# Paced weight preparation from step 0 to step 22 of the experts, and pools opened a step sooner, in a one-core attention, expert and gated-product kernel

## The chip, the cores and the metric

The kernel runs on one core of a Trainium2 chip. The metric is the device time of one execution in microseconds (us), median of several runs. The kernel before takes 837.07 us (three runs: 836.84, 837.07 and 842.2).

## The reference

Three layers follow each other. Linear attention gives x (2304 tokens, 512 features); a top-1 mixture of 8 experts replaces it; a gated product of three matrices gives the output.

```python
x = attn(q, k, v, w_phi)                      # linear attention, exp features
logits = x @ w_gate + modality_bias[modality_id]
e_idx = argmax(logits, axis=1)                # one expert for a token
for e in range(8):
    h = maximum(x[mask_e] @ w1[e], 0)         # 512 -> 1024
    out[mask_e] = gate_w * (h @ w2[e])        # 1024 -> 512
x = out
return ((x @ w_a) * (x @ w_b)) @ w_out        # 512 -> 1536 -> 512
```

The weights of the last layer come as 64-bit floats, laid out as pairs of 32-bit words.

## The kernel before

Every product is made of three matmuls on a high and a low part of both operands (`mm3`, lines 54 to 56). So each operand is split: ScalarE (ACT) copies it to the matmul's type, and VectorE (DVE) subtracts this copy from it.

**The experts** (`Moe.run`) work on four tiles of 608 tokens. A tile has eight steps. Steps 0 to 3 make the hidden layer: PE writes `hp`, ACT makes `hh` (L602), DVE makes `hl` (L603). Steps 4 to 7 make the output: PE writes `yp` from `hh` and `hl`, ACT copies it to `y` (L615). Together these are 32 steps, numbered 0 to 31. Each step has one slice of expert weights `s`, loaded by SyncE (SP, L555) and split two steps ahead into `wh` (ACT, L563) and `wl` (DVE, L564).

**The preparation** of the gated layer's weights runs beside the experts, as side jobs of these steps. The gated layer (`Moe2`) has 12 slices of weights; 10 of them (`NPRE`) are prepared during the experts, each in two halves, so there are 20 halves. A half has three jobs. `fetch` is a load of `raw` by SP (L700; three buffers). `clamp` is an absolute value on ACT (L708) and a maximum on GpSimd (POOL, L709). `narrow` is five DVE operations (L720, L722, L724, L725, L727) that turn the 64-bit words into 32-bit floats `wsum`. After the second half, `park` adds four small DVE operations (L736 to L739), and then splits the slice in two pieces of 1024 and 1280 columns: ACT writes `whi` (L744; one buffer), DVE subtracts it (L745), and SP stores both parts to DRAM as `wsc` (L746, L747).

A table `side` says at which step a job is handed to the scheduler. Inside `conv`, `high_priority(offset=-LOWP)` places the job's instructions as if they were written LOWP (200) instructions later; `issue_after(mo.act)` and `issue_after(mo.dve)` keep them behind the expert instruction that was handed over last on ACT and on DVE. Each engine then works through its instructions in the order so fixed.

**The boundary.** `open_first` is a side job too. It closes the preparation's buffers and opens the gated layer's in their place: `f_t`, `f_s` and `f_w0`. Into these go the prepared weights of slice 0, loaded back from `wsc` (`fw`, L774), and the sums and splits of the first tokens (`terms`: DVE `ysum` L806, ACT `yh` L791, DVE `yl` L792). All of them therefore wait until the last store of the preparation has left its buffer. Behind this stands a branch that all engines take (L1037; extra tiles, not needed with these inputs), and then the gated layer runs: PE makes the products `abp`, ACT copies them out (`pc`, L888). The last two slices of weights are prepared there, with loads of `raw` that SP issues behind the loads of the second slice's `fw`.

Of the kernel before, what the change touches and what calls it, by code (L numbers as in the profile page):

```python
# [37 lines left out]
NPRE = 10  # L38
LOWP = 200
LOWR = 80  # L40
LOWP2 = 60
# [7 lines left out]
def f32(ap):  # L49
    return ap.bitcast(F32)  # L50
# [213 lines left out]
def consts(nc, pool, keep, w_phi, w_gate):  # L264
    c = {}
    ident = c["ident"] = keep.tile([P, P], F32, name="ident")
    w = c["wp"] = pool.tile([P, P], F32, name="wp")
    nc.scalar.dma_start(out=w[0:64, :], in_=w_phi)
    nc.scalar.dma_start(out=w[64:128, :], in_=w_phi)
    make_identity(nc, ident)  # L270
    mask = c["mask"] = pool.tile([P, 2], F32, name="mask")
    wg = c["wg"] = pool.tile([P, 4, 16], F32, name="wg")
    nc.gpsimd.memset(wg, 0.0)
    src = w_gate.rearrange("(p h d) e -> h d p e", h=2, d=64)
    for h in range(2):
        rows = slice(64 * h, 64 * h + 64)
        nc.gpsimd.memset(mask[rows, h:h + 1], 0.0)
        nc.gpsimd.memset(mask[rows, 1 - h:2 - h], -1000.0)
        nc.gpsimd.dma_start(out=wg[rows, :, 8 * h:8 * h + 8], in_=src[h])
    return c  # L280
# [250 lines left out]
class Moe:  # L531
# [26 lines left out]
    def splitw(self, T, j):  # L558
        nc = self.nc
        src = T.pop(("st", j))  # L560
        hi = self.p_w.tile([P, 8, P], F32R, tag="h", name="wh")
        lo = self.p_w.tile([P, 8, P], F32R, tag="l", name="wl")
        nc.scalar.copy(hi, src)  # L563
        self.dve = nc.vector.tensor_sub(lo, src, f32(hi)).ins  # L564
        T["w", j] = (hi, lo)

# [360 lines left out]
def low(tc, step):  # L927
    def run():
        with tc.high_priority(offset=-LOWR):
            step()  # L930

    return run


@with_exitstack
def trn_kernel(ctx, tc, qk, v, vt, w_phi, mod_id, w_gate, bias, wm, wf, out):
    nc = tc.nc
    f64 = wf.dtype == mybir.dt.int64
    if f64:
        wf = wf.bitcast(I32)  # L940
    keep = ctx.enter_context(tc.tile_pool(name="keep", bufs=1))
    rpool = ctx.enter_context(tc.tile_pool(name="route", bufs=1))
    dpool = ctx.enter_context(tc.tile_pool(name="dram", bufs=1, space=bass.MemoryType.DRAM))
    xs = [dpool.tile([HALF, DM], F32, name=f"xs{i}") for i in range(2)]
    wsc = [[dpool.tile([P, 2304], F32, name=f"wsc{f}{j}") for j in range(2)] for f in range(Moe2.NF)]
    tl = dict(reuse_waits="tile")
    with ExitStack() as actx:
        cpool = actx.enter_context(tc.tile_pool(name="const", bufs=1))
        wkpool = actx.enter_context(tc.tile_pool(name="rwork", bufs=1))
        lgp = [(cpool, keep)[i].tile([P, NG, E], F32, name=f"lgp{i}") for i in range(2)]  # L950
        with tc.tile_pool(name="warm_ps", bufs=1, space=PSUM) as wps:
            z = cpool.tile([P, 512], BF16, name="warm")
            nc.vector.memset(z, 0.0)
            wz = wps.tile([P, 512], F32, name="warmp")
            for i in range(NWARM):
                nc.tensor.matmul(wz, z[:, :P], z, start=i == 0, stop=i == NWARM - 1)
        cst = consts(nc, cpool, keep, w_phi, w_gate)
        cst["warm"] = z
        at = Attn(nc, tc, actx, cst, qk, v, vt, xs, lgp)
        at.load(0)  # L960
        for r in range(9):
            if r + 1 < 8:
                at.load(r + 1)
            if r == 2:
                bs = bias_load(nc, cpool, keep, bias, mod_id)
                routes = [Route(tc, rpool, lgp[i], bs[i], i) for i in range(2)]
                rsteps = routes[0].steps(wkpool, at.ps_c, "c", at.first)
                rsteps = [low(tc, st) for st in rsteps[:6] + [lambda: routes[0].back(at.ps_q, "q")]]
            if r == 0:
                order = ExitStack()  # L970
                order.enter_context(tc.manual_schedule(engines={mybir.EngineType.PE}))
            at.round(r, {4: {2: rsteps[:1]}, 5: {0: rsteps[1:2], 2: rsteps[2:4]}, 6: {2: rsteps[4:5]}, 7: {0: rsteps[5:6]},
                         8: {0: rsteps[6:]}}.get(r, {}) if r > 2 else {})
            if r == 8:
                order.close()
    with ExitStack() as mctx:
        ps_t = mctx.enter_context(tc.tile_pool(name="ps_t", bufs=2, space=PSUM, **tl))
        ps_l = mctx.enter_context(tc.tile_pool(name="ps_l", bufs=3, space=PSUM, **tl))
        ypool = ctx.enter_context(tc.tile_pool(name="y", bufs=1, **tl))
        y = [ypool.tile([P, 4, YC], F32, name=f"y{i}") for i in range(2)]  # L980
        m2 = Moe2(nc, tc, wf, wsc, y, routes, out, f64)
        mo = Moe(nc, tc, mctx, cst, xs, wm, y, ps_l, ps_t)
        tiles = [(rt, t) for rt in routes for t in range(NTMIN)]
        rctx = ExitStack()
        cv = []
        nts = []
        ws = {}

        cctx = ExitStack()
        cv.append(cctx.enter_context(tc.tile_pool(name="cv", bufs=1, **tl)))  # L990

        def close_work():
            rctx.close()
            top = rpool.tile([1, 1], I32, name="top")
            n = slice(3 * NTMAX, 3 * NTMAX + 1)
            nc.vector.tensor_tensor(out=top, in0=routes[0].meta[:, n], in1=routes[1].meta[:, n], op=ALU.max)
            nts.append(nc.values_load(top[:, :], min_val=0, max_val=NTMAX))

        wk1 = rctx.enter_context(tc.tile_pool(name="rwork1", bufs=1, **tl))
        rs = routes[1].steps(wk1, ps_t, "t")  # L1000
        side = {}
        for f, k in enumerate((0, 0, 2, 4, 4, 8, 8)):
            side.setdefault(k, []).append(low(tc, rs[f]))
        side[9] = [close_work]

        def conv(f, half, job):
            def run():
                with tc.high_priority(offset=-LOWP), tc.issue_after(mo.act), tc.issue_after(mo.dve):
                    job(half)
            return run  # L1010

        K0, K1 = 2, len(tiles) * mo.NJ - 4
        for f in range(NPRE):
            fetch, clamp, narrow = m2.jobs(f, cv[0], 2, 3, 2)
            for half in range(2):
                k = K0 + (K1 - 2 - K0) * (2 * f + half) // (2 * NPRE)
                for i, job in enumerate((fetch, clamp, narrow)):
                    side.setdefault(k + i, []).append(conv(f, half, job))
        ts, src0 = {}, []

        def first():
            src, ts[0] = m2.terms(0, m2.p_s, ts.get(0), src0[0] if src0 else None)
            src0.append(src)

        def open_first():
            cctx.close()
            m2.p_t[0] = ctx.enter_context(tc.tile_pool(name="f_t", bufs=Moe2.NT0, **tl))
            m2.p_s = ctx.enter_context(tc.tile_pool(name="f_s", bufs=1, **tl))
            m2.p_w[0] = ctx.enter_context(tc.tile_pool(name="f_w0", bufs=1, **tl))
            ws[0] = m2.weights(0)  # L1030
            with tc.high_priority(offset=-LOWP):
                first()

        side.setdefault(K1, []).append(open_first)
        tc.mark_branch_hint_location("extra", "LikelyTaken", engines=ENGINES)
        mo.run(tiles, side, at)
        with tc.If(nts[0] > NTMIN, label="extra"):  # L1037
            n = slice(3 * NTMAX, 3 * NTMAX + 1)
            for rt in routes:
                extra(tc, mo, rt, nc.values_load(rt.meta[:, n], min_val=0, max_val=NTMAX))  # L1040
            first()
    cv.append(ctx.enter_context(tc.tile_pool(name="cv2", bufs=1, **tl)))
    side = {}
    for f in range(NPRE, Moe2.NF):
        for i, job in enumerate(m2.jobs(f, cv[1], 1, 2, 2)):
            for half in range(2):
                side.setdefault(2 * (f - NPRE) + i, []).append(lambda job=job, half=half: job(half))
    ps_l = ctx.enter_context(tc.tile_pool(name="ps_l2", bufs=2, space=PSUM, **tl))
    ps_a = ctx.enter_context(tc.tile_pool(name="ps_a2", bufs=1, space=PSUM, **tl))
    m2.pools(ctx, ps_a, ps_l)  # L1050
    m2.p_o = cv[1]
    m2.run(ws, ts, src0[0], side)
# [58 lines left out]
```

## Time and profile before

| | us |
|---|---|
| median of three runs | 837.07 |
| the profiled execution, its own time | 834.7 |
| its span in the trace | 832.9 |
| PE busy | 801.8 (96%) |
| DVE busy | 600.9 (72%) |
| ACT busy | 376.0 (45%) |
| POOL busy | 135.9 (16%) |

PE is TensorE's matmul queue, and PEclk (or the clock of a window) is the share of full speed that the chip granted it: 1.00 is 2.4 GHz, about 0.5 is 1.2 GHz. A timeline row gives the start, the duration, the engine, the line and the operation, with the tile written and the tiles read; in brackets stands the engine's idle time ahead of the row and what ended it. The experts run from about 163 to 388 us.

### The profile page before, as it was taken

The numbers are of one execution on the slowest core, as the hardware profiler recorded it, in microseconds if no ns is written. First come the engines' busy times: TensorE is split into PE (matmuls) and PEld (weight loads), VectorE is DVE, ScalarE is ACT, GpSimd is POOL, SyncE is SP. The second block draws the span as 40 slices with busy tenths as digits, with TensorE's granted clock in tenths as the row PEclk, the third lists the DMA queues.
The fourth block names the chain that finished last, engine by engine and source line by source line (L and its number), as shares of the span: only waits on it lengthen the run. The fifth ranks groups of instructions, "written<-read, shape, count | busy, mean of one in ns | idle before, by whom it ended". The sixth has DMA issues, their size and how long they took to land.

```text
span 832.9 us, 18335 instructions
## 1 busy us (share of the span) xinstructions
PE 801.8 (96%) x7283; PEld 754.7 (91%) x7284; DVE 600.9 (72%) x1071; ACT 376.0 (45%) x665; POOL 135.9 (16%) x164
## 2 busy tenths in 40 slices
PE   8999999899999999996699999999999999999996
PEld 6999888899999999996698999999999999999995
DVE  6888998759999999995698755775544686445553
ACT  4556555533545555542544433553333364333332
POOL 1000019403256232220022000030000002000002
PEclk9999999999999999999799999999999999999999
DMA  8665533753789977854888865576666668665632
GB/s 293 212 191 164 163 95 94 194 201 115 259 266 328 354 278 263 308 204 184 318 300 307 316 227 198 196 259 222 216 202 202 186 219 286 206 201 184 224 126 89
DMA packets 85163, 184.22 MB, mean 221 GB/s; under 512 B 27760, under 2 KB 37520, under 8 KB 85072
## 3 DMA queue, kind: packets, MB, share of 16 engines
q1 hardware_dynamic: 81872, 173.21, 61.6%
q0 software_dynamic: 3040, 9.72, 3.4%
q8 instruction: 58, 0.95, 0.5%
q14 instruction: 33, 0.27, 0.1%
q10 hardware_dynamic: 160, 0.07, 0.0%
HBM read 145.21 MB, written 37.75 MB: 220 GB/s over the span
## 4 chain that ended last, share of the span: by engine, by line
PE 32%; issue 16%; ACT 1%; DMA 1%; DVE 1%; POOL 0%; SPq 0%; POOLq 0%; DVEq 0%; ACTq 0%
PE abp L54 7%; PE abp L56 7%; PE abp L55 7%; PE op L56 4%; PE op L55 4%; PE op L54 4%; DMA raw<-in_moe_w 1%; ACT pc L888 0%; POOL out L844 0%; SPq L774 0%; DVE gl L876 0%; ACT gh L875 0%; DVE ca L874 0%; ACT yh L791 0%; DVE o L841 0%
## 5 line engine op out<-in xcount | busy, mean ns | idle before, releaser
L888 ACT COPY pc<-abp 128x384 f32<-128x384 f32 x252 | 120.7, 480 | 203.1 <-PE abp L56 199.2
L54 PE MATMUL abp<-yh,fw 128*128 128x384 f32 x504 | 171.9, 341 | 15.5 <-DVEq L1037 12.2
L56 PE MATMUL abp<-yh,fw 128*128 128x384 f32 x504 | 171.3, 340 | 0.0
L55 PE MATMUL abp<-yl,fw 128*128 128x384 f32 x504 | 171.2, 340 | 0.0
L54 PEld LDWEIGHTS abp<-yh,fw 128*128 128x128 f32 x504 | 95.7, 190 | 25.3 <-issue 12.4
L55 PEld LDWEIGHTS abp<-yl,fw 128*128 128x128 f32 x504 | 95.9, 190 | 7.4
L56 PEld LDWEIGHTS abp<-yh,fw 128*128 128x128 f32 x504 | 95.7, 190 | 0.0
L709 POOL TENSOR_SCALAR cvs<-cvs 128x768 f32<-128x768 f32 x24 | 62.0, 2583 | 188.6 <-ACT cvs L708 182.8
L55 PE MATMUL op<-fw,gh 128*128 128x512 f32 x216 | 85.9, 398 | 0.0
L54 PE MATMUL op<-fw,gh 128*128 128x512 f32 x216 | 85.4, 396 | 0.0
L56 PE MATMUL op<-fw,gl 128*128 128x512 f32 x216 | 85.3, 395 | 0.1
L54 PE MATMUL hp<-mxh,wh 128*128 128x304 f32 x256 | 78.0, 305 | 1.5 <-DVE x L242 1.5
L844 POOL DMA_INDIRECT out<-o,perm x18 | 18.4, 1020 | 367.6 <-ACT o L843 361.2
L55 PE MATMUL hp<-mxl,wh 128*128 128x304 f32 x256 | 77.7, 304 | 0.0
L56 PE MATMUL yp<-hh,wl 128*128 128x304 f32 x256 | 77.5, 303 | 0.0
L56 PE MATMUL hp<-mxh,wl 128*128 128x304 f32 x256 | 77.5, 303 | 0.0
L55 PE MATMUL yp<-hl,wh 128*128 128x304 f32 x256 | 77.3, 302 | 0.0
L54 PE MATMUL yp<-hh,wh 128*128 128x304 f32 x256 | 77.0, 303 | 0.0
L190 ACT ACTIVATE qts<-qtp 128x512 f32<-128x512 f32 (+1 forms) x80 | 38.3, 557 | 52.4 <-PE qtp L187 52.4
L899 DVE TENSOR_TENSOR d<-u,pc 128x768 f32<-128x768 f32 x36 | 34.4, 957 | 31.9 <-ACT pc L888 31.6
L876 DVE TENSOR_TENSOR gl<-ca,gh 128x384 fp32r<-128x384 f32 x72 | 39.8, 558 | 19.0 <-ACT gh L875 15.6
L156 DVE TENSOR_REDUCE m<-pjp 128x8 f32<-128x1024 f32 (+2 forms) x49 | 45.0, 933 | 10.9 <-PE pjp L154 10.9
(189 smaller groups left out, 1585.9 us busy)
## 6 DMA issues: line engine op xcount, KB each, us to landing
fw<-wsc SPq DMA_DIRECT2D x72, 512.0 KB, 4.3
fw<-wsc SPq DMA_DIRECT2D x144, 256.0 KB, 3.3
raw<-in_moe_w SPq DMA_DIRECT2D x24, 768.0 KB, 5.4
s<-in_moe_w SPq DMA_DIRECT2D x32, 512.0 KB, 6.3
fw<-wsc SPq DMA_DIRECT2D x72, 128.0 KB, 4.0
wsc<-whi SPq DMA_DIRECT2D x12, 640.0 KB, 6.8
wsc<-wsum SPq DMA_DIRECT2D x12, 640.0 KB, 7.4
wsc<-whi SPq DMA_DIRECT2D x12, 512.0 KB, 2.6
```

The lines of the kernel that those rows point to most:

```text
L54: nc.tensor.matmul(out, lh, rh, start=start, stop=False)
L55: nc.tensor.matmul(out, lh, rl, start=False, stop=False)
L56: return nc.tensor.matmul(out, ll, rh, start=False, stop=stop).ins
L156: nc.vector.tensor_reduce(out=mv, in_=pv, op=ALU.max, axis=AX.X, apply_absolute_value=True)
L190: nc.scalar.activation(t[:, s, :n, :], ps[:, :n, :], AF.Exp, scale=1.0 - 2.0 * s)
L709: nc.gpsimd.tensor_scalar(out=s.bitcast(F32), in0=s.bitcast(F32), scalar1=LEAST, scalar2=None, op0=ALU.max)
L844: st = nc.gpsimd.indirect_dma_start(out=self.out[:, :], out_offset=bass.IndirectOffsetOnAxis(ap=self.routes[bp].perm[:, c:c + 1], axis=0), ...
L876: nc.vector.tensor_sub(gl, ca[:, i, :], f32(gh))
L888: copied = nc.scalar.copy(x, ps).ins
L899: nc.vector.tensor_add(d, u, x.unsqueeze(1).to_broadcast([P, 2, n]))
```

## The change

Five things change in the side jobs, and no instruction is added or taken away.

- The 20 halves are handed over from step 1 on with an end at 24 in the formula (before: from step 2, with an end at 26). With the integer division the narrowing of the first half is at step 1 and that of the last at step 22 (before: 4 and 26).
- `narrow` stands at step k, `clamp` at k-1 and `fetch` at k-2 (before: k+2, k+1 and k).
- The jobs' place in the order is shifted by LOWP2 (60) in place of LOWP (200).
- `splitw` notes its `wh` cast as the latest ACT instruction, so that a job handed over behind it stays behind that cast.
- `open_first` is handed over at step 27 (before: 28).

```diff
-        nc.scalar.copy(hi, src)
+        self.act = nc.scalar.copy(hi, src).ins
...
-                with tc.high_priority(offset=-LOWP), tc.issue_after(mo.act), tc.issue_after(mo.dve):
+                with tc.high_priority(offset=-LOWP2), tc.issue_after(mo.act), tc.issue_after(mo.dve):
...
-        K0, K1 = 2, len(tiles) * mo.NJ - 4
+        K0, K1 = 1, len(tiles) * mo.NJ - 8
...
-                k = K0 + (K1 - 2 - K0) * (2 * f + half) // (2 * NPRE)
-                for i, job in enumerate((fetch, clamp, narrow)):
-                    side.setdefault(k + i, []).append(conv(f, half, job))
+                k = K0 + (K1 - K0) * (2 * f + half) // (2 * NPRE)
+                for i, job in ((2, fetch), (1, clamp), (0, narrow)):
+                    side.setdefault(max(k - i, 0), []).append(conv(f, half, job))
...
-        side.setdefault(K1, []).append(open_first)
+        side.setdefault(K1 + 3, []).append(open_first)
```

Three places show how the order of the engines moves. The first is DVE in the first steps of the experts' first tile. Before, no preparing row stands there; the rows end with the first of the routing sums:

```order
L564 TENSOR_TENSOR wl<-s,wh 128x1024
L603 SCALAR_TENSOR_TENSOR hl<-hp,hh 128x608 x2
L564 TENSOR_TENSOR wl<-s,wh 128x1024
L603 SCALAR_TENSOR_TENSOR hl<-hp,hh 128x608 x2
L564 TENSOR_TENSOR wl<-s,wh 128x1024
L603 SCALAR_TENSOR_TENSOR hl<-hp,hh 128x608
L398 COPY R<-rkp 128x80
```

In the changed kernel, DVE at the same place, from the same `wl` on:

```order
L564 TENSOR_TENSOR wl<-s,wh 128x1024
L603 SCALAR_TENSOR_TENSOR hl<-hp,hh 128x608
L720 TENSOR_SCALAR cvt<-cvs 128x768
L722 SCALAR_TENSOR_TENSOR cvt<-raw,cvt 128x768
L603 SCALAR_TENSOR_TENSOR hl<-hp,hh 128x608
L724 TENSOR_SCALAR cvs<-cvt 128x768
L725 SCALAR_TENSOR_TENSOR cvs<-raw,cvs 128x768
L727 TENSOR_TENSOR wsum<-cvt,cvs 128x768
L564 TENSOR_TENSOR wl<-s,wh 128x1024
```

A half's narrowing now stands between the first steps' splits, and another one follows behind the next `wl`. From here on the preparation is ahead of where it was: up to the third tile's last `hl` but one (its seventh of eight) DVE has 101 preparing rows ahead of it, before 87.

The second place is DVE at the experts' end, from the last expert split (`wl`) to the boundary. Before:

```order
L564 TENSOR_TENSOR wl<-s,wh 128x1024
L727 TENSOR_TENSOR wsum<-cvt,cvs 128x768
L745 TENSOR_TENSOR wsum<-wsum,whi 128x1280
L720 TENSOR_SCALAR cvt<-cvs 128x768
L722 SCALAR_TENSOR_TENSOR cvt<-raw,cvt 128x768
L724 TENSOR_SCALAR cvs<-cvt 128x768
L725 SCALAR_TENSOR_TENSOR cvs<-raw,cvs 128x768
L727 TENSOR_TENSOR wsum<-cvt,cvs 128x768
L736 TENSOR_TENSOR wsum<-wsum 128x256
L737 TENSOR_TENSOR wsum<-wsum 128x256
L738 TENSOR_TENSOR wsum<-wsum 128x256
L739 TENSOR_TENSOR wsum<-wsum 128x256
```

In the changed kernel, from the same `wl` to the first sum of the gated layer:

```order
L564 TENSOR_TENSOR wl<-s,wh 128x1024
L736 TENSOR_TENSOR wsum<-wsum 128x256
L737 TENSOR_TENSOR wsum<-wsum 128x256
L738 TENSOR_TENSOR wsum<-wsum 128x256
L739 TENSOR_TENSOR wsum<-wsum 128x256
L745 TENSOR_TENSOR wsum<-wsum,whi 128x1024
L745 TENSOR_TENSOR wsum<-wsum,whi 128x1280
L806 TENSOR_TENSOR ysum<-y_3069 128x768 x2
```

Seven rows (L727, the 1280-column L745 and a whole narrowing) have moved from behind the last `wl` to ahead of it; behind the four small rows both kernels go on with the same two L745 and the sums. On ACT, the last slice's two `whi` casts stand behind the third and the fourth of the last tile's eight `y` copies, where they stood behind the sixth and the seventh.

The third place is ACT right behind the branch, from the first copy of a gated product on (`raw` is the late slices' load, `gh` the split of the first gated value). Before:

```order
L888 COPY pc<-abp 128x384
L791 CAST yh<-ysum 128x768
L888 COPY pc<-abp 128x384
L791 CAST yh<-y_3069 128x768
L888 COPY pc<-abp 128x384 x5
L708 ACTIVATE cvs<-raw 128x768
L875 CAST gh<-ca 128x384
L888 COPY pc<-abp 128x384
```

In the changed kernel:

```order
L888 COPY pc<-abp 128x384
L791 CAST yh<-ysum 128x768
L888 COPY pc<-abp 128x384
L791 CAST yh<-y_3069 128x768
L888 COPY pc<-abp 128x384 x4
L708 ACTIVATE cvs<-raw 128x768
L888 COPY pc<-abp 128x384
L875 CAST gh<-ca 128x384
```

The clamp of the late slices' first half has moved ahead of the seventh product's copy. SP's order is the same in both kernels behind the branch.

## Rows read from the trace of the kernel before

**Rows 1.** The page's head: span of the profiled execution.
```profile
span 832.9 us, 18335 instructions
```
**Rows 2.** Windows: stretch, PE, PEld, DVE, ACT, POOL busy (instructions), PEclk, DMA share, GB/s.
```profile
280.00:300.00 20.00, 20.00 (x146) 20.00 (x145) 19.88 (x25) 11.46 (x15) 4.59 (x2) 1.00 0.89 305
320.00:340.00 20.00, 20.00 (x148) 20.00 (x147) 19.03 (x25) 10.25 (x16) 8.21 (x3) 1.00 0.85 288
```
**Rows 3.** Timeline of PE around the boundary: start, us, instruction [idle before <-releaser].
```profile
388.04 0.30 PE L56 MATMUL yp<-hh,wl 128*128 128x304 f32 x1
400.49 0.66 PE L54 MATMUL abp<-yh,fw 128*128 128x384 f32 x1 [12.16 <-DVEq L1037]
...
415.56 0.45 PE L54 MATMUL abp<-yh,fw 128*128 128x384 f32 x1 [2.88 <-ACT pc L888]
```
**Rows 4.** Windows of 1 us at the boundary, columns as in the second group.
```profile
392.00:393.00 1.00, 0.00 (x0) 0.00 (x0) 0.00 (x0) 0.00 (x0) 0.00 (x0) 0.67 0.03 10
405.00:406.00 1.00, 1.00 (x4) 1.00 (x4) 0.64 (x3) 0.92 (x2) 0.00 (x0) 0.51 0.92 373
```
**Rows 5.** Timeline of DVE from the last expert split to the boundary.
```profile
371.08 1.21 DVE L564 TENSOR_TENSOR wl<-s,wh 128x1024 fp32r<-128x1024 f32 x1
372.22 0.94 DVE L727 TENSOR_TENSOR wsum<-cvt,cvs 128x768 f32<-128x768 f32 x1
...
378.89 0.43 DVE L736 TENSOR_TENSOR wsum<-wsum 128x256 f32<-128x256 f32 x1
...
386.66 1.49 DVE L745 TENSOR_TENSOR wsum<-wsum,whi 128x1280 fp32r<-128x1280 f32 x1 [4.20 <-ACT whi L744]
...
393.02 0.96 DVE L806 TENSOR_TENSOR ysum<-y 128x768 f32<-128x768 f32 x1 [4.00 <-DMA wsc<-wsum]
```
**Rows 6.** Timeline of ACT at the experts' end.
```profile
367.56 1.06 ACT L744 CAST whi<-wsum 128x1024 fp32r<-128x1024 f32 x1 [1.92 <-DVE wsum L738]
...
368.82 1.05 ACT L563 CAST wh<-s 128x1024 fp32r<-128x1024 f32 x1
...
372.02 1.27 ACT L744 CAST whi<-wsum 128x1280 fp32r<-128x1280 f32 x1 [1.84 <-DMA wsc<-whi]
...
385.36 1.27 ACT L744 CAST whi<-wsum 128x1280 fp32r<-128x1280 f32 x1
```
**Rows 7.** Timeline of SP's queue of DMAs at the experts' end.
```profile
368.64 0.32 SPq L746 DMA_DIRECT2D wsc<-whi  x1
...
388.18 0.32 SPq L747 DMA_DIRECT2D wsc<-wsum  x1
393.02 13.99 SPq L774 DMA_DIRECT2D fw<-wsc  x16
```
**Rows 8.** Timeline of DVE in the first tile, up to the first preparing row.
```profile
175.87 0.79 DVE L603 SCALAR_TENSOR_TENSOR hl<-hp,hh 128x608 fp32r<-128x608 f32 x1 [1.14 <-ACT hh L602]
179.50 1.23 DVE L564 TENSOR_TENSOR wl<-s,wh 128x1024 fp32r<-128x1024 f32 x1 [2.84 <-ACT wh L563]
...
196.74 0.55 DVE L720 TENSOR_SCALAR cvt<-cvs 128x768 int32<-128x768 int32 x1
```
**Rows 9.** The chain that ended last, behind the branch: start, us, what.
```profile
402.83 0.49 ACT pc L888
...
407.05 6.76 DMA raw<-in_moe_w
...
414.63 0.50 ACT gh L875
...
416.00 0.17 PE abp L55
```
**Rows 10.** Timeline of SP's queue: the preparation's first loads.
```profile
163.45 1.04 SPq L700 DMA_DIRECT2D raw<-in_moe_w  x2
```
**Rows 11.** The page's part 6: issues of raw, KB each, median us to landing.
```profile
raw<-in_moe_w SPq DMA_DIRECT2D x24, 768.0 KB, 5.4
```
**Rows 12.** Timeline of DVE: the third tile's seventh hl.
```profile
303.76 0.77 DVE L603 SCALAR_TENSOR_TENSOR hl<-hp,hh 128x608 fp32r<-128x608 f32 x1
```
**Rows 13.** Timeline of PE: the first matmul that reads this hl.
```profile
308.81 0.30 PE L55 MATMUL yp<-hl,wh 128*128 128x304 f32 x1
```

## The prediction, made before the changed kernel ran

> **What bounds the kernel now.** I read the windows first. In a stretch of 20 us amid the experts PE is busy without a break, at the full clock, and DVE is busy 19.88 us of the 20; even in a loose stretch it is 19.03 [rows 2]. So there PE is the bound and DVE runs almost beside it: the kernel can't win there, but it could lose, if DVE's work for PE came late.
>
> Then I looked in PE's timeline for the breaks. The experts' last matmul starts at 388.04 and lasts 0.30, so it ends at 388.34; the next starts at 400.49, after 12.16 us of idle, put down to the branch on DVE's queue [rows 3]. A second break of 2.88 us ends at 415.56 [rows 3]. The clock falls in the first break, to 0.67 in the window at 392, and at 405 it is still 0.51, the lower level [rows 4]. These 15 us are all that a new order of the side jobs can win.
>
> What holds PE there is read backwards. DVE's second `ysum` starts at 393.02, released by the store of `wsum` [rows 5], and SP's sixteen `fw` loads start at the same moment [rows 7]. That last store was issued at 388.18 [rows 7]. The L745 in front of it began at 386.66 after waiting 4.20 for its `whi` [rows 5], a cast that ACT began at 385.36 [rows 6]. So the boundary is late because the last weight slice is prepared late.
>
> **What the change moves, step by step.** No instruction is added or removed. In the order, seven preparing rows go from behind the last `wl` to ahead of it. In the trace they are the rows from 372.22 up to 378.89, which is 6.67 us [rows 5].
>
> *Where they go.* DVE must have room for them earlier. In the first tile it idles twice for 1.14 and twice for 2.84 us (the rows at 175.87 and 179.50, and two more like them one step later) before its first preparing row at 196.74 [rows 8]: 2 x 1.14 + 2 x 2.84 = 7.96 us. The order puts a narrowing between just these splits. Its data is there in time: the first loads of `raw` are issued at 163.45 [rows 10] and land 5.4 us later by the median [rows 11], about 169; clamp and maximum add a few us before the first gap at about 175. So the last `wl` comes at 371.08 + 6.67 - 7.96 = 369.8. Its `wh` bounds it: begun at 368.82 and 1.05 long [rows 6], it ends at 369.87. I take 369.9, and 371.1 for the end of the 1.21 us row.
>
> *The tail that is left.* Four small rows at 0.43 [rows 5]: 1.7, to 372.8. The first `whi` (1.06 [rows 6]): 373.9, where its store is issued. `whi` has one buffer, so the second cast waits until that store has landed. In the trace the like store was issued at 368.64 [rows 7] and the next `whi` began at 372.02, released by it [rows 6]: 3.38 us. So 377.3; the second cast takes 1.27 [rows 6], to 378.55; its L745 takes 1.49 [rows 5], to 380.05, when the last store is issued. ACT's `y` copies are not in the way: in the new order the second cast stands behind the fourth copy instead of the seventh. Against 388.18 the last store is **8.13 us earlier**.
>
> *From there to PE.* The store took 388.18 to 393.02, 4.84 us, until sums and loads began, and from 393.02 to PE's 400.49 there are 7.47 us of sums, splits and first `fw`. Neither is changed; their data, `y` of the first tokens, is long there. So PE restarts at 380.05 + 4.84 + 7.47 = 392.4 rather than 400.49, and its gap is 4.0 us.
>
> A sentence by itself on this landing: the Trainium skill, page "DMA: Bandwidth & Descriptors", section "Anatomy of one DMA — SWDGE (gpsimd) path", gives about 2.0 us fixed, mostly the write receipt, plus the bytes at 436 GB/s; for a piece of 0.655 MB that is an estimate of 3.5 us, in place of the row's 4.84, and by it the gain would be 1.3 us larger, 8.7. The shorter store's 3.38 us is near the page's estimate (3.2 us), the last one is not.
>
> From rows alone the landing is bounded by 3.38 (an earlier start by 1.5 us) and 4.84; I take 4.84, which is the same store.
>
> *Behind the branch.* SP's eight loads for the second slice begin only after the first copy `pc` (402.83) and end at 407.05, where the late slices' `raw` is issued; that lands 6.76 us later and frees the clamp at 413.8, then `gh` at 414.63 and PE at 415.56 [rows 3, 9]. All of it starts from PE's restart, so it moves along as it is and the 2.88 us stay. The changed order costs a little: the clamp that waits for `raw` now has one product's copy more behind it, six matmuls at 0.17 to 0.18 us [rows 9], 1.05, less about 0.35 because `gh` (0.50) no longer stands ahead of that copy: **+0.7**. The bounds are 0 (PE finds other work) and 2.1 (the same at the lower clock).
>
> *The clock.* It fell about 4 us after PE's last matmul, and PE has the lower clock for some 5 us after the restart [rows 4]. With a gap of 4.0 us I expect a fall of nearly the same cost. What a quicker PE would win is in any case waited off at `raw`; I count nothing, with 0 to -2.6 (half of 5.2 us) as bounds.
>
> *The opening one step sooner* I cost at nothing: its sums and loads wait for the last store, and that is later than step 27 in either kernel. If that cover is gone, they start sooner and the gap is shorter.
>
> *DVE's work for PE.* Here the change could cost. Up to the third tile's seventh `hl` there are 101 preparing rows ahead, before 87. Fourteen rows at 19.88/25 = 0.795 us [rows 2] are 11.1 us; less the 7.96 of idle that is filled, this `hl` is 3.2 us later. With the mean of the seven rows (6.67/7 = 0.95) it is 13.3 - 7.96 = 5.4. It was ready at 304.53 [rows 12] and first read at 308.81 [rows 13], a slack of 4.28. So I cost it at nothing; the upper bound is 1.1 us a tile end, 3.3 for three of them.
>
> **Sum.** -8.13 + 0.7 = -7.4. The profiled execution takes 834.7 us (span 832.9 [rows 1], the rest lies around it), so 827.3. The median is 2.4 us above it at 837.07; I shift it by the same amount: **829.7 us**.
>
> **The rivals.**
>
> *R1: the gap nearly closes.* DVE's small waits in the middle (0.97 us in one stretch of 20 [rows 2]) are filled too, by jobs that lie ready earlier, or the loads land in 3.38. For: both are in the rows. Against: the last `wl` is held by its `wh`. With 3 us more, PE restarts at 389.4 and the time is 837.07 - 10.4 = 826.7.
>
> *R2: the change doesn't do what it says.* The last slice is not ready sooner, because ACT or the single `whi` buffer holds it, or because the early idle isn't filled, and the boundary is where it was. For: the 4.20 us wait came from ACT's order. Against: the new order has this cast three copies sooner. Then the gain is 0 to 1: about 836.5.
>
> *R3, on the other side: PE stalls on a late `hl`.* The preparing rows now have a smaller shift, so they stand ahead of `hl` rows that PE needs at the end of a tile's hidden layer. At 11.1 us of added rows, if none of the early idle were filled, each of three tile ends would stall by 11.1 - 4.28 = 6.8 us, 20 in all, less 7.4: slower by 13, 850. The price passes 1% from (8.4 + 7.4)/3 + 4.28 = 9.5 us of lateness on. Against: the idle is there, and the data is there before it.
>
> *R4: swallowed behind the branch.* The restart is sooner, but `raw` lands later, for its loads then meet the `fw` loads at another moment, and the second break grows by 2 to 4 us: 832 to 834, say 833.
>
> A change of 1% (8.4 us) is about what a measurement of this kernel can tell from none.
>
> **Chances.** The forecast (gain of 5 to 10 us, 827 to 832) 0.59; R1 0.15; R2 0.12; R4 0.06; R3 0.08. Faster by over 1% (below 828.7) are R1 and two fifths of the forecast: 0.15 + 0.24 = 0.39. Slower by over 1% is R3: 0.08. The rest, 0.53, is within 1%. The range goes from R1 with a little more, 825 (all of the gap), to 837 (no change); R3 and a part of R2 lie outside.
>
> **What would show it.** In the changed profile: DVE rows L720 to L727 in the gaps at 175 to 187; the last `wl` near 370, and behind it only four small rows and two L745; the last store issued near 380; PE's restart near 392.4 with about 4 us of idle ahead; a second break of 3 to 4 us some 15 us later, released by the clamp. PE busy without a break from 180 to 388. Wrong would be: `hl` rows that release PE at the tile ends (R3), a last `wl` still near 371 or a store still near 388 (R2), a restart before 390 (R1), a second break above 5 us (R4).

## The result and the profile after

The changed kernel takes 831.62 us (median of 12 runs), the kernel before, measured beside it, 841.17 us (12 runs). The ratio is 0.9888, with a 95% interval of 0.9866 to 0.9911: 1.1% faster, or 9.4 us, between 7.5 and 11.3. The forecast was 7.4 us. All comparisons below are such ratios, since the median of the same kernel before lay between 835.7 and 842.0 us from one set of runs to the next.

The profiled execution of the changed kernel took 832.25 us, with this head, whose row of before stands in [rows 1]:

```profile
span 830.5 us, 18343 instructions
```

(The counts differ by one matmul record and by instructions that only wait.) That is only 2.4 us less than before. But in this execution attention, which the change doesn't touch, ended some 8 us later. The experts' first `hp` matmul starts at 171.40 (before: 163.09), after PE's queue had waited six times for nothing that the profile shows (2.8 us in all) and the clock had been at 0.50 around 150 us. So the two traces are compared from the experts' end: 396.29 in this one, 388.34 in the one before. From there to the end of the span it is 434.2 us in this trace and 444.6 before, 10.4 less, while the experts take 224.9 and 225.3. So the gain lies behind the experts' end.

PE's timeline around the boundary, as [rows 3] of before:

```profile
395.99 0.30 PE L56 MATMUL yp<-hh,wl 128*128 128x304 f32 x1
398.07 0.41 PE L54 MATMUL abp<-yh,fw 128*128 128x384 f32 x1 [1.77 <-DVEq L1037]
...
410.58 0.69 PE L54 MATMUL abp<-yh,fw 128*128 128x384 f32 x1 [3.90 <-ACT pc L888]
```

The first break went from 12.16 to 1.77 us; the second grew from 2.88 to 3.90. DVE in the first tile, against [rows 8]:

```profile
184.31 0.78 DVE L603 SCALAR_TENSOR_TENSOR hl<-hp,hh 128x608 fp32r<-128x608 f32 x1
185.01 0.55 DVE L720 TENSOR_SCALAR cvt<-cvs 128x768 int32<-128x768 int32 x1
185.59 0.96 DVE L722 SCALAR_TENSOR_TENSOR cvt<-raw,cvt 128x768 int32<-128x768 int32 x1
186.47 0.78 DVE L603 SCALAR_TENSOR_TENSOR hl<-hp,hh 128x608 fp32r<-128x608 f32 x1
```

The first preparing row stands 13.6 us after the experts' first matmul (171.40), where before it stood 33.7 us after it (196.74 and 163.09), and none of these rows shows a wait. DVE's busy time in the experts' first 40 us, before and then in the changed kernel (stretch, DVE busy, PEclk, DMA share, GB/s), grew by 7.0 us, about the 6.67 of the seven rows:

```profile
163.09:203.09 40.00, 29.33 (x93) 1.00 0.47 157
171.40:211.40 40.00, 36.35 (x80) 1.00 0.73 246
```

On ACT the early start shows already. The first load of `raw`, issued at 171.76, released its clamp only 7.4 us later, and the first `hh` stands behind this clamp:

```profile
179.19 0.90 ACT L708 ACTIVATE cvs<-raw 128x768 f32<-128x768 f32 x1 [6.42 <-DMA raw<-in_moe_w]
...
180.14 0.67 ACT L602 ACTIVATE hh<-hp 128x608 fp32r<-128x608 f32 x1
```

It began 8.74 us after the experts' first matmul, before 6.85 (169.94); PE did not stall for it. At the experts' end DVE, SP and ACT look like this (against [rows 5 to 7]):

```profile
377.41 1.23 DVE L564 TENSOR_TENSOR wl<-s,wh 128x1024 fp32r<-128x1024 f32 x1 [0.61 <-ACT wh L563]
378.55 0.42 DVE L736 TENSOR_TENSOR wsum<-wsum 128x256 f32<-128x256 f32 x1
...
385.04 1.49 DVE L745 TENSOR_TENSOR wsum<-wsum,whi 128x1280 fp32r<-128x1280 f32 x1 [2.77 <-ACT whi L744]
...
389.67 0.96 DVE L806 TENSOR_TENSOR ysum<-y 128x768 f32<-128x768 f32 x1 [2.27 <-DMA wsc<-wsum]
...
394.19 0.96 DVE L792 TENSOR_TENSOR yl<-ysum,yh 128x768 fp32r<-128x768 f32 x1 [1.47 <-ACT yh L791]
```
```profile
381.04 0.32 SPq L746 DMA_DIRECT2D wsc<-whi  x1
...
386.56 0.32 SPq L747 DMA_DIRECT2D wsc<-wsum  x1
389.66 12.74 SPq L774 DMA_DIRECT2D fw<-wsc  x16
```
```profile
379.96 1.05 ACT L744 CAST whi<-wsum 128x1024 fp32r<-128x1024 f32 x1
...
383.74 1.26 ACT L744 CAST whi<-wsum 128x1280 fp32r<-128x1280 f32 x1 [0.29 <-DMA wsc<-whi]
...
393.01 0.41 ACT L615 COPY y<-yp 128x304 f32 x1 [2.15 <-PE yp L56]
393.32 0.84 ACT L791 CAST yh<-ysum 128x768 fp32r<-128x768 f32 x1
...
409.26 0.89 ACT L708 ACTIVATE cvs<-raw 128x768 f32<-128x768 f32 x1 [4.17 <-DMA raw<-in_moe_w]
```

From here on, times counted from the experts' end carry a sign. The last `wl` starts at -18.88 (before -17.26), the last store is issued at -9.73 (before -0.16), `ysum` and the first `fw` start at -6.6 (before +4.7), and PE restarts at +1.78 (before +12.15). PE's clock, in windows as in [rows 4]:

```profile
396.00:398.00 2.00, 0.30 (x3) 0.05 (x1) 1.75 (x3) 0.77 (x2) 0.00 (x0) 1.00 0.77 277
...
409.00:410.00 1.00, 0.00 (x0) 0.00 (x0) 0.00 (x0) 0.73 (x1) 0.00 (x0) 0.50 0.97 397
...
414.00:415.00 1.00, 1.00 (x4) 0.92 (x3) 1.00 (x3) 0.12 (x1) 0.46 (x1) 0.50 0.81 265
```

Behind the short first break it stays at full speed; behind the second it is at the lower level for about 6 us.

### The profile page after: what moved, and what is told of

It is laid out like the page before. It is cut to its first block, busy times and chain, and to the rows that moved or that the text cites. A ratio compares the mean times of both kernels' runs of the same rounds, so it can differ in the third digit from the quotient of the medians.

```text
span 830.5 us, 18343 instructions
## 1 busy us (share of the span) xinstructions
PE 805.1 (97%) x7284; PEld 756.5 (91%) x7284; DVE 599.8 (72%) x1071; ACT 375.6 (45%) x665; POOL 130.5 (16%) x164
## 3 DMA queue, kind: packets, MB, share of 16 engines
q0 software_dynamic: 3040, 9.72, 3.4%
## 4 chain that ended last, share of the span: by engine, by line
issue 46%; POOL 2%; PE 2%; DMA 1%; SPq 0%; ACT 0%; POOLq 0%
POOL out L844 2%; DMA raw<-in_moe_w 1%; POOL cvs L709 1%; SPq L774 0%; PE abp L54 0%; PE abp L56 0%; PE abp L55 0%; PE op L55 0%; PE op L54 0%; PE op L56 0%; POOLq L1108 0%; ACT pc L888 0%; ACT cvs L708 0%; POOLq L844 0%
## 5 line engine op out<-in xcount | busy, mean ns | idle before, releaser
L709 POOL TENSOR_SCALAR cvs<-cvs 128x768 f32<-128x768 f32 x24 | 58.7, 2446 | 169.7 <-ACT cvs L708 169.6
L844 POOL DMA_INDIRECT out<-o,perm x18 | 18.4, 1020 | 372.3 <-ACT o L843 365.3
L875 ACT CAST gh<-ca 128x384 fp32r<-128x384 f32 x72 | 36.8, 515 | 36.2 <-DVE ca L874 36.2
```

Of the source, the lines that this page charges most:

```text
L709: nc.gpsimd.tensor_scalar(out=s.bitcast(F32), in0=s.bitcast(F32), scalar1=LEAST, scalar2=None, op0=ALU.max)
L844: st = nc.gpsimd.indirect_dma_start(out=self.out[:, :], out_offset=bass.IndirectOffsetOnAxis(ap=self.routes[bp].perm[:, c:c + 1], axis=0), ...
L875: nc.scalar.copy(gh, ca[:, i, :])
```

## The experiments

My theory after the result: the gain comes from DVE's idle in the first tile. DVE is nearly full afterwards (99.31 of the next 102.20 us up to the third tile's seventh `hl`, 97%), so what is filled in early comes off the end, whatever the plan says later. What is left is a second break that is ACT's. The first four runs take the change apart; diffs are against the changed kernel where nothing else is said.

| run | ratio to the kernel before (95%) | first break, us | second break, us | last store from the experts' end, us |
|---|---|---|---|---|
| before, its trace | 1 | 12.16 | 2.88 | -0.16 |
| changed, its trace | 0.9888 (0.9866 to 0.9911) | 1.77 | 3.90 | -9.73 |
| start4 | 1.0001 (0.9982 to 1.0019) | 12.32 | 2.33 | -0.16 |
| pace28 | 0.9897 (0.9873 to 0.9922) | 1.77 | 5.18 | -9.73 |
| pace_only | 0.9893 (0.9868 to 0.9918) | 1.77 | 4.38 | -9.73 |
| dve_late | 0.9921 (0.9895 to 0.9948) | 7.87 | 1.55 | -3.06 |
| after2 | 0.9871 (0.9845 to 0.9897) | 1.77 | 6.16 | -9.72 |
| yh_first | 0.9893 (0.9862 to 0.9925) | 1.20 | 4.85 | -9.74 |
| clamp_late | 0.9801 (0.9775 to 0.9828) | 1.77 | 0.75 | -9.73 |
| clamp_yh | 0.9823 (0.9793 to 0.9852) | 1.20 | none | -9.73 |
| before_clamp | 0.9952 (0.9931 to 0.9973) | 12.21 | none | -0.16 |
| clamp_start0 | 0.9814 (0.9786 to 0.9842) | 1.02 | none | -13.38 |
| npre9_clamp | 0.9824 (0.9797 to 0.9851) | 1.02 | none | -27.55 |

**The start or the end of the plan?** Two runs put one number each back.

```diff
-        K0, K1 = 1, len(tiles) * mo.NJ - 8
+        K0, K1 = 4, len(tiles) * mo.NJ - 8      # start4: first narrowing at step 4, last at 23
```

> The changed kernel with one number put back: the first narrowing stands at step 4 again (as in the kernel before), the last still at an early step (23). Theory (the gain comes from DVE's idle in the first tile, which only an early start can fill, since DVE is full afterwards): nothing is won, the time is that of the kernel before within 2 us, PE's first break is 11 to 13 us and seven preparing rows stand behind the last wl. Rival A (the earlier end of the plan, or the smaller shift of the jobs, or the opening a step sooner brings the last slice forward): 8 to 10 us faster than before, first break about 2 us.

```diff
-        K0, K1 = 1, len(tiles) * mo.NJ - 8
+        K0, K1 = 1, len(tiles) * mo.NJ - 4      # pace28: first at step 1, last at 26
-        side.setdefault(K1 + 3, []).append(open_first)
+        side.setdefault(27, []).append(open_first)
```

> The changed kernel with the other number put back: the first narrowing at step 1, the last at step 26, as late as in the kernel before. Theory (the start decides, not the end): the full gain, 8 to 11 us faster than before, first break 1 to 3 us, last store issued as in the changed kernel relative to the experts' end. Rival A (the end of the plan decides): within 2 us of the kernel before.

Without the early start nothing that is measured was left of the gain, and DVE is busy 29.45 us of the experts' first 40, as before; without the early end all of the gain was left. PE's timeline of start4, then of pace28:

```profile
400.99 0.66 PE L54 MATMUL abp<-yh,fw 128*128 128x384 f32 x1 [12.32 <-DVEq L1037]
```
```profile
389.94 0.41 PE L54 MATMUL abp<-yh,fw 128*128 128x384 f32 x1 [1.77 <-DVEq L1037]
```

**The shift of the jobs and the opening.** The changed pace alone, with the `wh` cast as a mark (a job at step 0 needs one), with the larger shift and the opening at step 28:

```diff
-                with tc.high_priority(offset=-LOWP2), tc.issue_after(mo.act), tc.issue_after(mo.dve):
+                with tc.high_priority(offset=-LOWP), tc.issue_after(mo.act), tc.issue_after(mo.dve):
-        side.setdefault(K1 + 3, []).append(open_first)
+        side.setdefault(K1 + 4, []).append(open_first)
```

> The changed pace and the wh cast as a mark, but the jobs keep the larger shift (200) and the pools open at step 28. Theory (with an early start DVE's idle is filled whatever the shift): 8 to 11 us faster than before, first break 1 to 3 us. Rival B (the smaller shift puts the early rows there): under 3 us faster, first break over 8 us. And if the rows with the smaller shift cost PE anything at the tile ends, this kernel is faster than the changed one; by the theory it is the same within 2 us.

It has the gain and the breaks of the changed kernel. So the smaller shift and the earlier opening are worth nothing that is measured. With the opening at 28 alone put back, the order of every engine is the same as in the changed kernel; with the larger shift too, it differs in six places on DVE, two on ACT and eleven on PE, so this run tests the shift no further than that.

**Is DVE's work what the end waits for?** Ten repeats of one DVE operation were added in the second tile:

```diff
-        nc.vector.tensor_scalar(out=t, in0=s, scalar1=3, scalar2=0x3FFFFFF8,
+        for _ in range(11 if (f, half) == (4, 0) else 1): nc.vector.tensor_scalar(out=t, in0=s, scalar1=3, scalar2=0x3FFFFFF8,
```

> The changed kernel with one DVE operation (L720 of the ninth half) repeated ten times with the same result: 10 x 0.55 = 5.5 us of DVE work added in the second tile. Theory (DVE is full from step 1 on, so each us of its work shows at the end): the last wl stays, four preparing rows more stand behind it, the last store is 3 to 5 us later against the experts' end, and the time is 3 to 5 us above the changed kernel, so 4 to 7 below the one before; PE doesn't stall at the tile ends. Rival C (the tail is bound by casts and store landings, DVE has room): the same as the changed kernel within 1 us. Rival D (hl rows come late and PE stalls at the tile ends): a stall of about 5.5 - 2.4 = 3 us at a tile end in the trace.

The last store is 6.7 us later and the first break 6.1 us longer, and PE doesn't stall at a tile end. PE's waits of this run, from the experts' begin to 30 us behind their end (what waits, for what: us in total, times, longest):

```profile
PE abp L54 <- DVEq L1037: 7.9, 1, 7.9
PE abp L54 <- ACT pc L888: 1.5, 1, 1.5
PE hp L54 <- DVE x L242: 1.4, 1, 1.4
```

So rivals C and D fall: 5.5 us of work cost 6 us at the boundary. But the time rose only by some 0.3% (2 to 3 us, with intervals that overlap), less than the 3 to 5 us expected: the second break shrank to 1.5 us. PE worked at the lower clock (0.50 from 395 to 399) behind the longer first break, and so ran out of work later; and in this order the late clamp stands behind eight product copies and a `gh`, where the changed kernel has it behind six copies. That pointed at the second break.

**A second trace of the changed kernel, and two edits on the second break.**

> The changed kernel as it is, once more, for a second trace of it. Theory (the 8 us by which attention ends later in its first trace belong to that one execution): the experts start near 163 us as in the kernel before, the span is 821 to 824 us, PE's first break is 1.8 us and its second 3.5 to 5.5; 8 to 11 us faster than before. Rival E (the change itself delays attention): the experts start near 171 us again.

The first break is 1.77 us again, the second 6.16, longer than expected. The experts started at 167.3 us, between the two theories. In the four traces of this set of runs they started between 167 and 171 us, in kernels that differ only behind the attention; the traces of start4, pace28, pace_only and dve_late have 162 to 164, with the changed start or not, and the three of the last set 162 to 167. So the change doesn't cause it. The wait of PE's queue for nothing that the profile shows (2.6 to 2.8 us in all) stands in both traces of the changed kernel and in the other three of this set, and in none of the eight other traces. The kernel before, measured beside, took 841 to 842 us in these two sets and 836 in the others, so it is slower there too; the ratio takes that out. What holds PE's queue I didn't find out.

```diff
-            self.act = nc.scalar.copy(self.y[T["rt"].bp][:, m, ds(T["s"][g], CG)], ps).ins
+            with self.tc.issue_after(self.hold) if m == 3 and getattr(self, "hold", None) else nullcontext(): self.act = ...
...
-                first()
+                first(); mo.hold = m2.cast      # the last yh cast
```

> The changed kernel with the last two y copies of the experts put behind the gated layer's first yh casts on ACT. By the term of the prediction (everything behind the branch starts from PE's restart): the yl rows no longer wait for casts behind a y copy, PE restarts 0.9 us sooner, and the time falls by 0.9 us. Rival F (the loads of raw start from SP's branch, not from PE): the first break shrinks by 0.9 to about 0.8 us, the second grows by as much, and the time stays.

The first break shrank by 0.57 us, to 1.20, now released by the branch on ACT's queue; the time did not change beyond the interval. The loads of `raw` were issued 6.48 us after the experts' end, as in pace_only (6.49), with PE's restart 0.57 us sooner. So rival F holds: they don't start from PE. Two traces of the same kernel show it more clearly. In the changed kernel's first trace and in after2 PE restarts 1.8 us after the experts' end, but `raw` is issued 4.38 and 6.52 us after that restart. SP's own waits at the branch, in the first and in the second (us in total, times, longest):

```profile
SPq L1037 <- SPq L1037: 4.7, 4, 3.7
```
```profile
SPq L1037 <- SPq L1037: 6.8, 4, 3.9
```

What SP waits for there can be read from the landings in the trace. Each load lands in 16 parts; the last part of slice 0's eight `fw` loads landed at 398.17 and at 396.42, and the first load behind the branch was issued 0.56 and 0.57 us later (398.73, 396.99). In all traces but the last two of the table this distance is 0.56 or 0.57 us. Those eight loads start when the last store has landed. So `raw` hangs on that store and on the landing of SP's own loads, not on PE; in twelve traces (without npre9_clamp) it was issued 12.8 to 14.9 us after the first of them. In after2 the last part came 1.8 us behind the one before it, in the changed kernel's first trace 0.03, and this is most of the difference between their second breaks (6.16 and 3.90).

```diff
-            with self.tc.high_priority(offset=-LOWP2):
+            with self.tc.high_priority(offset=-LOWP2), self.tc.issue_after(self.pcs[-4]) if k else nullcontext():
                 for st in side.get(k, ()):
...
-                side.setdefault(2 * (f - NPRE) + i, []).append(...)
+                side.setdefault(2 * (f - NPRE) + i + (i > 0), []).append(...)
```

(`pcs` is the list of product copies so far.)

> The changed kernel with the late slices' clamps moved one step later and behind the fourth product copy of the second slice on ACT. Theory (the second break is ACT's queue: pc copies and gh behind a clamp that waits for raw): the break of 3.9 us and the fall of the clock behind it (5 us at the lower level, about 2.5 us) vanish, 4 to 7 us faster than the changed kernel, 13 to 17 faster than before. Rival G (PE would wait there for the second slice's fw in any case, which land at the same moment as raw): a break of 2 to 4 us stays, released by a DMA of fw, and under 2 us are won.

This has the lowest ratio of the table: 2.0% faster than the kernel before. (The three runs below that keep this edit on the changed kernel, 0.9814 to 0.9824, can't be told from it.) ACT behind the branch in this run:

```profile
409.86 0.48 ACT L888 COPY pc<-abp 128x384 f32<-128x384 f32 x1 [1.22 <-PE abp L56]
410.24 0.92 ACT L708 ACTIVATE cvs<-raw 128x768 f32<-128x768 f32 x1
413.45 0.90 ACT L708 ACTIVATE cvs<-raw 128x768 f32<-128x768 f32 x1 [2.29 <-DMA raw<-in_moe_w]
414.25 0.85 ACT L888 COPY pc<-abp 128x384 f32<-128x384 f32 x2
```

The first clamp now finds `raw` landed; the second still waits 2.29, of which 0.75 reach PE. No window of 1 us up to 430 shows a clock under 1.00. Rival G falls: no `fw` took the place of `raw`.

Both edits together:

> Both edits together: the late clamps behind the copies, and the last two y copies behind the yh casts. Theory: with the second break gone, the 0.9 us of the earlier restart show in the time: 0.5 to 1.2 us faster than the late clamps alone, first break about 0.8 us, 14 to 18 us faster than before. Rival G as before: a break released by fw, and no more than 3 us better than the changed kernel.

The second break is gone, but the ratio is not better than that of clamp_late (the intervals overlap by most of their width). The 0.57 us can't be told from nothing in the time.

**Is the second break a cost of its own?** The same edit on the kernel before:

> The kernel before, with only the late clamps moved behind the copies as in the run clamp_late. Theory (the second break and the fall of the clock behind it are a cost of their own, in the kernel before too): the break of 2.9 us and about 1.6 us of the 3.2 us at the lower clock vanish, 3 to 6 us faster than before; the first break stays at 12 us. So the change's gain and this one add up: the changed kernel with the late clamps lies 9 to 12 us below this one. Rival H (the early restart is what lets the late clamps pay): under 2 us faster.

0.5% (4.0 us) faster, with the first break as it was and the second gone; rival H falls. From here the change with the late clamps gains another 1.5% (some 13 us, give or take 3), where 9 to 12 were expected.

**How much further?** One number more in the same direction, on clamp_late:

```diff
-        K0, K1 = 1, len(tiles) * mo.NJ - 8
+        K0, K1 = 0, len(tiles) * mo.NJ - 8
```

> The changed kernel with the late clamps, and the first narrowing at step 0 in place of 1 (five more preparing rows ahead of the last wl). Theory (the rest of the first break, 1.8 us, is no longer DVE's work but yh, yl and the branch): the last store is 4 to 6 us earlier against the experts' end, the first break shrinks only to about 1 us, the time is 0 to 1.5 us below the run clamp_late. Rival D (rows moved still further ahead make hl late and PE stalls at the tile ends): PE breaks of 1 us or more at a tile end, slower than clamp_late by 1 us or more.

Here the price of an early start shows. DVE and then PE in the first tile:

```profile
177.04 0.56 DVE L720 TENSOR_SCALAR cvt<-cvs 128x768 int32<-128x768 int32 x1 [2.16 <-POOL cvs L709]
...
178.91 1.39 DVE L722 SCALAR_TENSOR_TENSOR cvt<-raw,cvt 128x768 int32<-128x768 int32 x1
...
180.30 0.78 DVE L603 SCALAR_TENSOR_TENSOR hl<-hp,hh 128x608 fp32r<-128x608 f32 x1
```
```profile
181.13 0.41 PE L54 MATMUL hp<-mxh,wh 128*128 128x304 f32 x1 [1.66 <-DVE hl L603]
```

The first narrowing is queued before its data is ready: DVE waits 2.16 us for POOL's maximum, with an `hl` behind it, and PE stalls 1.66 us for that `hl` (and 0.32 later). ACT is held too: the second clamp waits for its load with the first `hh` behind it, which begins at 178.63, 11.24 us after the experts' first matmul:

```profile
177.67 0.90 ACT L708 ACTIVATE cvs<-raw 128x768 f32<-128x768 f32 x1 [2.91 <-DMA raw<-in_moe_w]
```

Which of the two waits made the `hl` late isn't parted. The last store came 3.65 us earlier (4 to 6 were expected), the first break shrank to 1.02, and the experts took 228.2 us, 2.5 more than in clamp_late: and the time is that of clamp_late within the intervals, which are too wide to tell 1 us. So both were half right: the break shrank as the theory said, and rival D's stall is there, in the first tile rather than at a tile end.

One slice fewer beside the experts, on clamp_late:

```diff
-NPRE = 10
+NPRE = 9
```

> The changed kernel with the late clamps, and one slice fewer prepared beside the experts (9, so three are prepared in the gated layer). It takes 12 us of DVE work from the experts. Theory (what is left of the first break is the branch itself): the last store is over 20 us earlier, all yl are done before the experts' end, and the first break is still 0.5 to 1.2 us; the time is within 2 us of clamp_late, since the gated layer has DVE time to spare (60% busy) for the third slice. Rival I (a preparation in the gated layer costs PE as it did at its begin): 3 us or more slower than clamp_late.

The last store is 27.55 us ahead of the experts' end, and PE still pauses:

```profile
389.59 0.44 PE L54 MATMUL abp<-yh,fw 128*128 128x384 f32 x1 [1.02 <-ACTq L1037]
```

So 1.02 us stay when all of the preparation is done early, and of the 1.77 in the changed kernel only 0.75 is late work. The 1.02 is not the branch alone: ACT's last `y` copy, which has to wait for PE's last expert product, stands in it with 0.41 us:

```profile
388.66 0.41 ACT L615 COPY y<-yp 128x304 f32 x1 [2.96 <-PEq L1037]
```

The third slice in the gated layer cost nothing that is measured.

## Why the prediction was right, and where its terms were off

The direction, the mechanism up to PE's restart and the time were right: 829.7 was forecast, 831.62 measured, in the range. That the two times lie so near is in part luck: the kernel before, measured beside, took 841.17 and not 837.07, 4.1 us more, and the gain was 2.0 us larger than forecast. Of the rivals, R1 (the gap nearly closes, 10.4 us) lies nearest to the measured 9.4: its quicker landing came true, and the restart at 1.78 us after the experts' end is within 0.7 us of its 389.4. Point by point:

- **The bound** (the last slice prepared late): right; start4 and dve_late show the first break going with the last store.
- **DVE's early idle takes the seven rows**: right, and it is the whole gain (start4, pace28; 7.0 us more of DVE work in the first 40). The last `wl` was forecast at 369.9, which is -18.4 from the experts' end, and stands at -18.88. That the data is there in time was right for step 1, but closer than I had it: `raw` released its clamp 7.4 us after its issue, not 5.4, and held ACT for 6.42. clamp_start0 shows it false one step earlier.
- **The tail up to the last store**: forecast at 380.05, or -8.29; measured -9.73, a term 1.4 us too large. I had set the first `whi` behind all four small rows, but it began at 379.96 while the last of them still ran. And the landing between the two casts took 2.70 us (381.04 to 383.74), not 3.38.
- **The last landing**: I took 4.84; it took 3.10 (386.56 to 389.66). I chose the same store's row; the lower bound, 3.38, would have been the better value. 15 of the store's 16 parts landed after 2.99 us before and 2.95 now; before, the last one came 1.73 us behind them (see the last section). The Trainium skill ("DMA: Bandwidth & Descriptors", section "Anatomy of one DMA — SWDGE (gpsimd) path") gives its fit for DMAs that GpSimd issues, and this store is SP's; the estimate of about 3.5 us by that fit is nearer to the 3.10 than the 4.84 was.
- **Sums and splits until PE**: 7.47 taken as unchanged; it took 8.41 (389.66 to 398.07). I missed that the new ACT order puts the sixth and the seventh `y` copy ahead of the `yh` casts: the first two `yl` waited 0.26 and 1.47 for their `yh`, before 0 and 0.90, which is 0.83 of the 0.94. I had named the order of the casts but only asked whether `whi` was held.
- Together: -1.44 - 1.74 + 0.94 makes -2.2, about what the first break is shorter than forecast (4.0 against 1.77).
- **Behind the branch** the step failed. "All of it starts from PE's restart" is wrong: SP's loads start when SP leaves the branch, and that is when its eight loads of slice 0 have landed. SP issued `raw` 4.38 and 6.52 us after PE's restart in two traces of the changed kernel, 6.56 in the one before. Nor do the second slice's loads "begin only after the first copy `pc`": in the changed kernel they begin at 398.73 and `pc` at 399.43, and in start4, with the first break of before, at 403.05 and 403.33. The second break did not stay at 2.88 but was 3.9 to 6.2 in four traces (after, after2, pace28, pace_only), part of it by the clamp moved one copy forward, as costed. It ate 1 to 3 us of the first break's 10.4. Two of the four (5.18, 6.16) are above the 5 us that I had named as the sign of R4. Its reason is not what happened: `raw` landed 6.8 to 7.0 us after its issue in these four and 6.8 before. The break grew because PE was through its products sooner after its restart (8.61 us, before 12.19), one product fewer and none at the lower clock, while `raw` was issued only 2.2 us sooner after the restart, in after2 not at all.
- **The clock**: I expected a fall behind the first break, as before. With 1.77 us of idle there was none; it fell at the second. clamp_late has neither. That a quicker PE wins nothing there, since it waits for `raw`, was right. (Before, the lower level lasted 5.5 us behind the restart, not 5.2.)
- **The opening at no cost**: right, and the smaller shift (which I had not priced by itself) is worth nothing that is measured either.
- **`hl` late at the tile ends** (R3): costed at nothing, and right. DVE and PE of the changed kernel at the third tile, against [rows 12, 13]:

```profile
313.60 0.78 DVE L603 SCALAR_TENSOR_TENSOR hl<-hp,hh 128x608 fp32r<-128x608 f32 x1
```
```profile
316.88 0.30 PE L55 MATMUL yp<-hl,wh 128*128 128x304 f32 x1
```

It is ready at 314.38 and read at 316.88: 2.5 us of slack, where my 4.28 and the 3.2 us of lateness would have left 1.1. Counted from the experts' first matmul this `hl` came 1.5 us later than before. R3's stall on a late `hl` does occur (clamp_start0), but in the first tile, where a queued row waits for its data, not at the tile ends.

## What to carry to other kernels

Where an engine is nearly full to the end, look for the idle at its begin: fill it as soon as the data is there, and not a step before, since a queued row that waits blocks what stands behind it. When a wait goes, look for the next one on the engines that were hidden by it: here a clamp that waited for a load, in front of copies that PE needed, cost 0.5% (before_clamp) to some 0.9% (clamp_late). And check for each load what releases its issue: "behind PE's restart" and "behind the landing of the queue's own earlier loads" looked alike in one trace and parted in the next.

## What the runs showed of the hardware that I had not expected

**A store that lands late for one of its 16 parts.** Until the loads began behind it, the same store took 3.1 to 3.2 us when it was issued 3 to 10 us ahead of the experts' end (changed kernel 3.10, dve_late 3.22), 3.80 us when it was issued 13.4 us ahead (clamp_start0), and 4.8 to 5.0 us when it was issued 0.16 us ahead (before 4.84, start4 5.00, before_clamp 4.78). In all six, 15 of its 16 parts had landed after 2.95 to 3.01 us; what differs is the last one. In the trace before the DMA engines are nearly full until 390.6, and then a share of 0.06, about one engine of 16, works on until 392.3:

```profile
391.00:392.00 1.00, 0.00 (x0) 0.00 (x0) 0.00 (x0) 0.00 (x0) 0.00 (x0) 1.00 0.06 26
```

The last part landed at 392.90, 1.73 us behind the others, and the buffer counts as free only then. The list of DMA packets shows what ran beside the store. From 387 to 393 in the trace before (queue and kind: packets, MB, share of 16 engines):

```profile
q1 hardware_dynamic: 288, 1.31, 54.1%
q8 instruction: 1, 0.02, 1.6%
```

and from 386 to 390 in the changed kernel, around its store:

```profile
q1 hardware_dynamic: 272, 1.23, 75.3%
```

The packet of kind `instruction` has 16384 bytes; it started at 387.44, 0.74 us ahead of the store's issue, and took 1.56 us. In start4 and before_clamp such a packet started 0.71 and 0.72 us ahead of the store's issue and took 1.69 and 1.48 us, and the last part came 1.87 and 1.65 us behind the others. In clamp_start0 one of 0.96 us started 1.47 us ahead, and the last part came 0.71 us behind. In the eight other traces with ten slices none started between 5 us ahead of the store's issue and 2.7 us behind it, and the last part came at most 0.1 us behind. So these instruction packets fit the delay in size and in time. That they held the very engine that was late the trace doesn't say, and no run moved such a packet by itself; this cause is likely and not shown.

**Where the clock fell.** In two traces it fell only when PE was working again: in start4 PE idled 2.33 us until 415.52, and the windows from 417 to 420 show 0.50, the lower level; before, it idled 2.88 us until 415.56, and those from 417 to 419 do. In the changed kernel PE idled from 406.7 to 410.58, and the lower level lasts from 409 to 415. Behind the first break of the changed kernel (1.77 us) no window shows it.
